# A planned attention and gMLP kernel: a second y3 buffer, transfers counted by the planner, chunk 0's load and scan, and the last outputs begun in part

## The chip, the cores and the metric

The kernel runs on one core of a Trainium2 chip. The metric is the device time of one execution in microseconds (us); a kernel's time is the median of its runs.

## The reference

For 4 batches and 8 heads of 48 dimensions over 768 positions the reference runs gated linear attention, and puts the result through a gated MLP with a spatial product:

```python
for t in range(S):
    state = alpha[:, :, t, :, None] * state + np.einsum('bhd,bhe->bhde', k[:, :, t], v[:, :, t])
    y[:, :, t] = np.einsum('bhd,bhde->bhe', q[:, :, t], state)
...
x = np.ascontiguousarray(attn_out.transpose(0, 2, 1, 3)).reshape(B, S, H * D)
h = x @ w_in
h = 0.5 * h * (1.0 + np.tanh(c * (h + 0.044715 * h ** 3)))
u, v = (h[..., :d_ff // 2], h[..., d_ff // 2:])
v_n = (v - mu) / np.sqrt(var + 1e-06) * g_ln
v_s = np.einsum('ts,bsd->btd', w_sg, v_n) + b_sg[None, :, None]
gated = u * v_s
return (x + gated @ w_out).astype(np.float32)
```

All is float32; d_model is 384 and d_ff is 1024. `mu` and `var` are the mean and variance of `v` over its 512 columns.

## The kernel before

**Attention.** The sequence of each batch is cut into 6 chunks of 128 positions; there are 24 chunks, 0 to 23, and a batch with its MLP is called a block. Chunk `i` loads `a` (decays, `load_a`) and `kqv` (768 KB, `load_kqv`). VectorE (DVE) scans the decays forward (`decay`, L333), scales the queries with the result `pf` (`scale_q`, L343), scans backward (`invert`, L351, into `pf` again) and scales the keys (`scale_k`, L361); `floor` is a small tile that L347 and L357 set between the scans. TensorE (PE) then works in groups G(o, i): the scores of chunk i (`sc`, L376), the outputs of chunk o (`y`, L389 and L399) and o's products of keys and values (`dl`, L410). VectorE masks the scores (`causal`, L475) and keeps the state: `state_half` (L495, or the copy L497 in the first chunk of a block), `state_add` (L500) and `state_decay` (L503). The second half of `y` reads `s_m`, which `state_half` writes.

**Between the two.** ScalarE (ACT) copies a chunk's `y` into the rows of `xf` and its last part into `y3` (`y_last`, L507). Six small DMAs, the packs (L520), put `y3` into the rest of `xf`. Then `xf` is split into a high part `xh` (L528) and a low part `xl` (L532).

**MLP.** A float32 product is made of three matmuls of high and low parts (`mm3`, L549 to L551). V(b, c) and U(b, hf, d) are the products with `w_in`; P(b, hf, d) is the spatial product (`mm_s`, 18 matmuls), whose result VectorE takes up (L630, then the gate L635, on GpSimd or VectorE) and splits into `gh` (L640) and `gl` (L645); R(b, hf, kk) is the output product (`mm_o`, 12 matmuls, the terms d = 0 to 3), followed by the add L663 into a tile `r` with two buffers, and its store L667. During block 0 the weights are split too: pieces of `w_in` and `w_out` pass ACT L247, DVE L250 to L269, ACT L263 and the lines L277 to L287, pieces of `w_sg` pass ACT L223 and DVE L226.

**Order.** Every engine works its queue off in order. The order is made when the program is built, by a list scheduler (`class Plan`): each step has an engine, a cost in ns, the steps that it follows, the tiles that it takes (with how many buffers, and who must be done before one comes free) and a due time. PE's steps have a fixed sequence, `units`, of which a step may be at most `ahead` places early; the other engines take of what is ready the step that is due first. A step marked `dve*` or `pool` may not run in the plan beside one on the other of these two engines, and some steps may go to either. All DMAs are issued by SyncE (SP), in its queue's order. In the program, each of SP's DMAs waits until the eighth one before it has landed; in the plan nothing stands for that.

## Time and profile before

| | us |
|---|---|
| median of 3 runs | 375.91 |
| lowest and highest | 375.25, 377.3 |
| the profiled execution, its own time | 374.54 |
| its span in the trace | 372.8 |
| TensorE busy in the span | 344.4 |
| VectorE busy | 265.1 |
| ScalarE busy | 152.8 |
| GpSimd busy | 60.6 |

The span leaves out 1.74 us of the execution's own time. Block 0 lasts to about 131 us: up to there the attention of two blocks, the first MLP and the weights' split share the engines. From there on TensorE waits little. To read the rows further below: a bracket such as [3.59 <-ACT y L507] says that the engine stood idle for 3.59 us before the instruction, and which instruction's end it waited for.

### The profile page before, as it was taken

Reading aid. Unit: us, or ns where it says so; the run is one execution under the profiler, and the core shown is the slowest. Engines: PE = TensorE matmul, PEld = TensorE weight load, DVE = VectorE, ACT = ScalarE, POOL = GpSimd, SP = SyncE. Lnnn points to the kernel's source line nnn. Section 1 sums busy time; section 2 is a strip of 40 time slices with the busy share of each in tenths; the row PEclk is TensorE's granted clock in tenths of the full one; section 3 lists DMA queues with packets and bytes.
Section 4 is the critical chain, followed back from the end, with each engine's and each line's share of the span. In section 5 each row is a group of like instructions: output and inputs, shape, how many; then the busy total and the mean of one; then the engine's idle time right before and its main releaser. Section 6 shows DMA issues by size and latency. Waiting matters only on the chain.

```text
span 372.8 us, 10703 instructions
## 1 busy us (share of the span) xinstructions
PE 344.4 (92%) x4480; PEld 314.3 (84%) x4480; DVE 265.1 (71%) x526; ACT 152.8 (41%) x367; POOL 60.6 (16%) x103
## 2 busy tenths in 40 slices
PE   2786989999998799999999999899999999999993
PEld 2554768799998798989999998699999989799983
DVE  4799997799996977888466887786577645443351
ACT  3285576755433344653312445543232335311010
POOL 1002133414201121320101301420111113300000
PEclk9999699999999999999999999999999999999998
DMA  8855675125356134531232344131221110000102
GB/s 304 281 195 139 218 250 181 42 73 163 98 170 205 31 111 122 162 114 37 66 117 93 119 138 136 52 101 28 92 83 73 30 50 8 1 2 0 63 3 70
DMA packets 18712, 39.38 MB, mean 106 GB/s; under 512 B 3936, under 2 KB 10848, under 8 KB 18656
## 3 DMA queue, kind: packets, MB, share of 16 engines
q1 hardware_dynamic: 18656, 38.61, 32.2%
q8 instruction: 37, 0.61, 0.7%
q14 instruction: 19, 0.16, 0.1%
HBM read 32.70 MB, written 4.72 MB: 100 GB/s over the span
## 4 chain that ended last, share of the span: by engine, by line
PE 68%; DVE 10%; DMA 8%; ACT 4%; SPq 4%; issue 3%; POOL 2%; DVEq 0%; ACTq 0%; POOLq 0%
PE mm_s L551 8%; PE mm_s L549 8%; PE mm_s L550 8%; DMA xf<-y 4%; PE mm_o L550 4%; PE mm_o L551 4%; PE mm_o L549 4%; PE mm_u L549 4%; SPq L520 4%; PE mm_u L551 4%; PE mm_u L550 4%; PE mm_v L549 3%; DMA kqv_t<-in_kqv 3%; PE mm_v L551 3%; PE mm_v L550 3%
## 5 line engine op out<-in xcount | busy, mean ns | idle before, releaser
L549 PE MATMUL mm_s<-ws_hi,vh 128*128 128x384 f32 x192 | 65.9, 343 | 1.3 <-ACT ws_hi L223 0.8
L550 PE MATMUL mm_s<-ws_lo,vh 128*128 128x384 f32 x192 | 65.1, 339 | 0.4 <-DVE ws_lo L226 0.4
L551 PE MATMUL mm_s<-ws_hi,vl 128*128 128x384 f32 x192 | 65.1, 339 | 0.1
L640 ACT CAST gh<-g 128x384 fp32r<-128x384 f32 x32 | 16.3, 512 | 57.9 <-DVE g L635 39.4
L630 DVE SCALAR_TENSOR_TENSOR g<-mm_s,g_col,b_bc 128x384 f32<-128x384 f32 x32 | 19.4, 608 | 26.1 <-PE mm_s L551 26.1
L549 PEld LDWEIGHTS mm_s<-ws_hi,vh 128*128 128x128 f32 x192 | 36.0, 188 | 2.1 <-ACT ws_hi L223 1.1
L550 PEld LDWEIGHTS mm_s<-ws_lo,vh 128*128 128x128 f32 x192 | 36.1, 188 | 0.8 <-DVE ws_lo L226 0.7
L551 PEld LDWEIGHTS mm_s<-ws_hi,vl 128*128 128x128 f32 x192 | 36.0, 188 | 0.4 <-DVE vl L596 0.4
L376 PE MATMUL sc<-kqv_t 64*64 64x64 f32 x768 | 27.8, 231 | 7.4 <-DVE kqv_t L361 4.7
L549 PE MATMUL mm_u<-xh,wi_hi 128*128 128x384 f32 x96 | 33.2, 346 | 0.1
L549 PE MATMUL mm_o<-gh,wo_hi 128*128 128x384 f32 x96 | 32.4, 338 | 0.3 <-ACT gh L640 0.3
L376 PEld LDWEIGHTS sc<-kqv_t 64*64 64x64 f32 x768 | 25.4, 146 | 8.5 <-DVE kqv_t L361 5.1
L550 PE MATMUL mm_o<-gl,wo_hi 128*128 128x384 f32 x96 | 32.4, 338 | 0.1
L550 PE MATMUL mm_u<-xl,wi_hi 128*128 128x384 f32 x96 | 32.5, 338 | 0.0
L551 PE MATMUL mm_u<-xh,wi_lo 128*128 128x384 f32 x96 | 32.4, 338 | 0.0
L551 PE MATMUL mm_o<-gh,wo_lo 128*128 128x384 f32 x96 | 32.3, 337 | 0.0
L549 PE MATMUL mm_v<-wi_hi,xh 128*128 128x512 f32 x72 | 30.3, 421 | 1.7 <-ACT u L615 1.4
L333 DVE TENSOR_TENSOR_SCAN pf<-a,floor 128x516 f32<-128x516 f32 x24 | 30.0, 1251 | 2.4 <-DMA a<-in_aT 2.2
L351 DVE TENSOR_TENSOR_SCAN pf<-a,floor 128x516 f32<-128x516 f32 x24 | 29.5, 1228 | 1.1 <-ACT pend L339 0.4
L551 PE MATMUL mm_v<-wi_hi,xl 128*128 128x512 f32 x72 | 28.5, 396 | 0.0
L550 PE MATMUL mm_v<-wi_lo,xh 128*128 128x512 f32 x72 | 28.4, 395 | 0.0
L389 PEld LDWEIGHTS y<-at,kqv_t 64*64 64x64 f32 x768 | 16.9, 141 | 13.2 <-issue 5.3
(109 smaller groups left out, 760.2 us busy)
## 6 DMA issues: line engine op xcount, KB each, us to landing
kqv_t<-in_kqv SPq DMA_DIRECT2D x24, 768.0 KB, 4.6
a<-in_aT SPq DMA_DIRECT2D x24, 258.5 KB, 2.7
out_x<-r SPq DMA_DIRECT2D x24, 192.0 KB, 2.5
raw<-in_w_in SPq DMA_DIRECT2D x8, 384.0 KB, 8.0
xf<-y SPq DMA_DIRECT2D x144, 8.0 KB, 2.7
raw<-in_w_out SPq DMA_DIRECT2D x4, 384.0 KB, 3.3
raw<-in_w_sgT SPq DMA_DIRECT2D x6, 192.0 KB, 2.4
raw_sg<-in_w_sgT SPq DMA_DIRECT2D x1, 768.0 KB
```

Of the source, the lines that this page charges most:

```text
L333: nc.vector.tensor_tensor_scan(pf.rearrange("p j t -> p (j t)"), s["a"][:, 0:NP * C1], floor.rearrange("p j t -> p (j t)"), initial=0.0, o ...
L351: nc.vector.tensor_tensor_scan(s["pf"].rearrange("p j t -> p (j t)")[:, ::-1], s["a"][:, NP * C1:0:-1], floor.rearrange("p j t -> p (j t)" ...
L376: lambda j=j, h=h: nc.tensor.matmul(sc[half(h), e, 64 * j:64 * j + 64], k[half(e), j, half(h)], q[half(e), j, half(h)], start=True, stop=True,
L389: lambda j=j: nc.tensor.matmul(y_of(y, j, e)[:, half(h)], v[half(h), j, half(e)], at[half(h), e, j], start=first and j < 2, stop=True, ski ...
L520: nc.sync.dma_start(xf[64 * e + D:64 * e + 64, kk, tsl], y3[64 * e + 16 * kk:64 * e + 16 * kk + 16, :])
L549: nc.tensor.matmul(o, lh, rh, start=(idx == 0), stop=False)
L550: nc.tensor.matmul(o, lh, rl, start=False, stop=False)
L551: nc.tensor.matmul(o, ll, rh, start=False, stop=(idx == n - 1))
L630: nc.vector.scalar_tensor_tensor(t["g"], t["o"], g_col[:, d:d + 1], b_bc[:, tsl], op0=ALU.mult, op1=ALU.add,)
L640: nc.scalar.copy(g["h"][:, d], t["g"])
```

## The change

The change has six parts.

1. The planner holds a DMA back until the eighth one before it has landed in its model (`SLOTS`). Only the order of the queues changes by it.
2. `y3` has two buffers: the copy of chunk i no longer has to follow the six packs of chunk i - 1.
3. Chunk 0's load of `kqv` is cut in two, keys and queries first (512 KB), then values (256 KB).
4. Chunk 0's backward scan writes into a tile `ip`, which is taken out of `xf`'s buffers, and no longer follows the scaling of the queries. In the plan, `pf` comes free when both q and k are scaled.
5. The copy of `state_half` in the first chunk of a block (four times) goes from VectorE to ScalarE.
6. Of the last three output products, the first two are begun with their first three terms d (9 matmuls each, `begin`), ahead of the last term (3 matmuls, `end`) of either; the third follows whole. In every output product the last term's three matmuls now stand in the order hi by `gh`, lo by `gh`, hi by `gl`.

```diff
     RATE = 280.0
+    SLOTS = 8
...
                     t1 = max(t, free[e])
+                    if s["nbytes"] and len(landed) >= self.SLOTS:
+                        t1 = max(t1, landed[-self.SLOTS])
...
                 done[n] = dma + 1900
+                landed.append(done[n])
...
-        nc.sync.dma_start(kqv_t, kqv[i])
+        if i == 0:
+            nc.sync.dma_start(kqv_t[:, 0:2], kqv[i, :, 0:2])
+            nc.sync.dma_start(kqv_t[:, 2], kqv[i, :, 2])
+        else:
+            nc.sync.dma_start(kqv_t, kqv[i])
...
     def invert(i):
         s = st[i]
+        if i == 0:
+
+            s["ip"] = mlp.tile([P, NK, TH], F32, tag="xf", name="ip", bufs=3).rearrange("p k t -> p (k t)")[
+                :, 0:NP * C1].rearrange("p (j t) -> p j t", t=C1)
+        else:
+            s["ip"] = s["pf"]
         nc.vector.tensor_tensor_scan(
-            s["pf"].rearrange("p j t -> p (j t)")[:, ::-1], s["a"][:, NP * C1:0:-1],
+            s["ip"].rearrange("p j t -> p (j t)")[:, ::-1], s["a"][:, NP * C1:0:-1],
...
-            nc.vector.tensor_copy(smd, d0)
+            nc.scalar.copy(smd, d0)
...
-        st[i]["y3"] = y3 = att1.tile([P, C], F32, tag="y3", name="y3")
+        st[i]["y3"] = y3 = att1.tile([P, C], F32, tag="y3", name="y3", bufs=2)
...
+        def begin():
+            t["o"] = psm.tile([P, TH], F32, tag="mm", name="mm_o")
+            terms = [(wo_hi[:, d, sl], wo_lo[:, d, sl], g["h"][:, d], g["l"][:, d]) for d in range(ND - 1)]
+            mm3(t["o"], terms, whole=False)
+
+        def end():
+            d = ND - 1
+            for lh, rh in ((wo_hi, "h"), (wo_lo, "h"), (wo_hi, "l")):
+                nc.tensor.matmul(t["o"], lh[:, d, sl], g[rh][:, d], start=False, stop=(rh == "l"))
...
         def product():
-            t["o"] = psm.tile([P, TH], F32, tag="mm", name="mm_o")
-            mm3(t["o"], [(wo_hi[:, d, sl], wo_lo[:, d, sl], g["h"][:, d], g["l"][:, d]) for d in range(ND)])
+            begin()
+            end()
...
-            units += p(b, 1, 0) + r(b, 0) + p(b, 1, 1) + p(b, 1, 2) + p(b, 1, 3) + r(b, 1)
+            units += p(b, 1, 0) + r(b, 0) + p(b, 1, 1) + p(b, 1, 2) + p(b, 1, 3)
+            units += [(("R", b, 1, kk, "begin"), 1560) for kk in range(2)] + r(b, 1)
...
-        plan.add(("recip", i), "dve*", 1225, lambda i=i: invert(i), [("q", i), ("pend", i), ("end", i)])
+        plan.add(("recip", i), "dve*", 1225, lambda i=i: invert(i), ([("q", i)] if i > 0 else []) + [("pend", i), ("end", i)])
...
-            ("half", i), "dve", 350, lambda i=i: state_half(i), [o_at[i]],
+            ("half", i), "dve" if c > 0 else "act", 350, lambda i=i: state_half(i), [o_at[i]],
```

Where the change moves instructions, three places of the queues are shown, before and after. Line numbers of the changed kernel lie 5 to 30 higher, since lines were added.

VectorE in the head, chunk 0, before (`pf` and `floor` as told above):

```order
L333 SCALAR_TENSOR_TENSOR pf<-a,floor 128x516
L347 RECIPROCAL floor<-pf 128x4
L343 TENSOR_TENSOR kqv_t<-kqv_t,pf 128x512
L351 SCALAR_TENSOR_TENSOR pf<-a,floor 128x516
L357 MEMSET floor 128x4
L361 TENSOR_TENSOR kqv_t<-kqv_t,pf 128x512
L475 TENSOR_TENSOR at<-sc,mask 128x512
```

and after:

```order
L342 SCALAR_TENSOR_TENSOR pf<-a,floor 128x516
L356 RECIPROCAL floor<-pf 128x4
L366 SCALAR_TENSOR_TENSOR ip<-a,floor 128x516
L372 MEMSET floor 128x4
L376 TENSOR_TENSOR kqv_t<-kqv_t,ip 128x512
L352 TENSOR_TENSOR kqv_t<-kqv_t,pf 128x512
L490 TENSOR_TENSOR at<-sc,mask 128x512
```

The scaling of the queries (L343, after L352) moved from ahead of the backward scan to behind the scaling of the keys (L361, after L376).

SyncE around the packs of chunk 5, before (`xf<-y_832` are the packs of chunk 4, `xf<-y_936` those of chunk 5; `raw` is a piece of a weight):

```order
L322 DMA a<-in_aT 128x517
L520 DMA xf<-y_832 16x128 x6
L243 DMA raw<-in_w_in 128x768
L327 DMA kqv_t<-in_kqv 128x1536
L243 DMA raw<-in_w_in 128x768
L520 DMA xf<-y_936 16x128 x6
L243 DMA raw<-in_w_out 128x768 x2
```

and after:

```order
L965 DMA g_col<-in_g_ln 128x4
L336 DMA kqv_t<-in_kqv 128x1536
L327 DMA a<-in_aT 128x517
L535 DMA xf<-y_832 16x128 x6
L535 DMA xf<-y_915 16x128 x6
L248 DMA raw<-in_w_in 128x768 x2
L336 DMA kqv_t<-in_kqv 128x1536
L327 DMA a<-in_aT 128x517
L248 DMA raw<-in_w_out 128x768 x2
```

The packs of chunk 5 (after: `xf<-y_915`) moved ahead of the load of chunk 8's `kqv` and of both pieces of `w_in`, right behind those of chunk 4.

VectorE ahead of the first half of the state of chunk 7, which is the row `s_m<-s_c,dl_1451`, before:

```order
L347 RECIPROCAL floor<-pf 128x4
L635 TENSOR_TENSOR g<-g,u 128x384
L284 TENSOR_TENSOR top<-top,wo_hi 128x384
L266 TENSOR_SCALAR mag<-top 128x384
L269 SCALAR_TENSOR_TENSOR mag<-raw,mag 128x384 x2
L287 TENSOR_TENSOR wo_lo<-top,mag 128x384
L495 TENSOR_TENSOR s_m<-s_c,dl_1451 128x4x48
L475 TENSOR_TENSOR at<-sc,mask 128x512
L645 TENSOR_TENSOR gl<-g,gh 128x384 x2
L343 TENSOR_TENSOR kqv_t<-kqv_t,pf 128x512
```

and after, where it is the row `s_m<-s_c,dl_1466` (L645 is before's L630, L650 is L635, L660 is L645, L352 is L343, L366 is L351, L231 is L226, L292 is L287):

```order
L289 TENSOR_TENSOR top<-top,wo_hi 128x384
L645 SCALAR_TENSOR_TENSOR g<-mm_s,g_col,b_bc 128x384
L292 TENSOR_TENSOR wo_lo<-top,mag 128x384
L650 TENSOR_TENSOR g<-g,u 128x384
L352 TENSOR_TENSOR kqv_t<-kqv_t,pf 128x512
L231 TENSOR_TENSOR ws_lo<-raw,ws_hi 128x384
L660 TENSOR_TENSOR gl<-g,gh 128x384
L366 SCALAR_TENSOR_TENSOR pf<-a,floor 128x516
L510 TENSOR_TENSOR s_m<-s_c,dl_1466 128x4x48
L231 TENSOR_TENSOR ws_lo<-raw,ws_hi 128x384
L376 TENSOR_TENSOR kqv_t<-kqv_t,pf 128x512
L515 TENSOR_TENSOR s_m<-s_m,sc 128x4x48
```

The scaling of chunk 8's queries, its backward scan and a piece of `w_sg` moved from behind this row to ahead of it, two more low halves `gl` are done ahead of it, and a gate (L635) and three of the low parts of `w_out` (L287), which GpSimd made before, are VectorE's now.

## Rows read from the trace of the kernel before

**Rows 1.** The page, its row of busy times: busy us, share of the span and number of instructions of each engine.

```profile
PE 344.4 (92%) x4480; PEld 314.3 (84%) x4480; DVE 265.1 (71%) x526; ACT 152.8 (41%) x367; POOL 60.6 (16%) x103
```

**Rows 2.** The view by windows over the whole span, cut at the stages of block 0 and the rest: window, its length, then busy us (and instructions) of PE, PEld, DVE, ACT and POOL, the granted TensorE clock as a share of full speed, the busy share of the DMA engines, GB/s.

```profile
20.00:36.00 16.00, 13.24 (x290) 9.70 (x290) 15.29 (x30) 11.71 (x33) 1.88 (x1) 1.00 0.53 166
36.00:50.00 14.00, 11.86 (x263) 9.60 (x263) 13.83 (x27) 7.40 (x19) 1.72 (x1) 0.76 0.60 197
50.00:72.00 22.00, 20.41 (x176) 15.99 (x176) 17.65 (x43) 15.53 (x35) 9.16 (x16) 1.00 0.55 174
72.00:88.00 16.00, 16.00 (x116) 14.82 (x115) 15.67 (x34) 10.20 (x24) 3.52 (x4) 1.00 0.21 59
88.00:102.00 14.00, 14.00 (x301) 13.37 (x300) 13.32 (x31) 6.72 (x18) 4.95 (x4) 1.00 0.49 151
```

**Rows 3.** The same view in finer windows around TensorE's longest wait.

```profile
36.00:38.00 2.00, 0.00 (x0) 0.00 (x0) 2.00 (x6) 1.40 (x4) 0.12 (x1) 0.56 0.80 203
...
42.00:43.00 1.00, 1.00 (x5) 0.89 (x4) 1.00 (x1) 0.15 (x1) 0.00 (x0) 0.50 0.09 17
```

**Rows 4.** The timeline of VectorE in the head, chunk 0: start, duration, engine, line, operation, out<-in, shapes, count, and in brackets the idle time before it with what ended it.

```profile
5.09 0.18 DVE L347 RECIPROCAL floor<-pf 128x4 f32<-128x4 f32 x1
5.71 0.69 DVE L343 TENSOR_TENSOR kqv_t<-kqv_t,pf 128x512 f32<-128x512 f32 x1 [0.44 <-DMA kqv_t<-in_kqv]
6.51 1.23 DVE L351 TENSOR_TENSOR_SCAN pf<-a,floor 128x516 f32<-128x516 f32 x1
7.79 0.68 DVE L361 TENSOR_TENSOR kqv_t<-kqv_t,pf 128x512 f32<-128x512 f32 x1
```

**Rows 5.** The timeline of TensorE, the rows before which it waits and that the prediction speaks of (at 100.31 it doesn't wait).

```profile
8.53 0.70 PE L376 MATMUL sc<-kqv_t 64*64 64x64 f32 x16 [4.35 <-DVE kqv_t L361]
...
38.02 0.39 PE L389 MATMUL y<-at,kqv_t 64*64 64x64 f32 x4 [3.59 <-ACT y L507]
...
67.50 0.50 PE L549 MATMUL mm_v<-wi_hi,xh 128*128 128x512 f32 x1 [0.30 <-ACT xh L528]
...
100.31 0.41 PE L399 MATMUL y<-kqv_t,s_m 64*64 64x64 f32 x16
...
114.61 0.45 PE L549 MATMUL mm_s<-ws_hi,vh 128*128 128x384 f32 x1 [0.76 <-ACT ws_hi L223]
...
115.49 0.44 PE L550 MATMUL mm_s<-ws_lo,vh 128*128 128x384 f32 x1 [0.43 <-DVE ws_lo L226]
...
128.93 0.46 PE L389 MATMUL y<-at,kqv_t 64*64 64x64 f32 x16 [1.44 <-ACT alo L454]
...
130.22 0.46 PE L399 MATMUL y<-kqv_t,s_m 64*64 64x64 f32 x16 [0.59 <-DVE s_m L495]
```

**Rows 6.** The timeline of SyncE's queue of DMA issues, at the loads ahead of chunk 5's packs, and at the load of chunk 11.

```profile
57.73 0.52 SPq L243 DMA_DIRECT2D raw<-in_w_in  x1
...
110.62 1.84 SPq L220 DMA_DIRECT2D raw<-in_w_sgT  x2
...
113.02 0.38 SPq L327 DMA_DIRECT2D kqv_t<-in_kqv  x1
```

**Rows 7.** The timeline of ScalarE at chunk 5's y3 and xh.

```profile
59.15 0.27 ACT L507 COPY y<-y 128x128 f32<-128x128 f32 x1 [1.30 <-DMA xf<-y]
...
66.94 0.51 ACT L528 CAST xh<-xf 128x384 fp32r<-128x384 f32 x1 [1.37 <-DMA xf<-y]
```

**Rows 8.** The timeline of VectorE, at the first half of the state of chunk 7 and at the queries of chunk 11.

```profile
99.61 0.35 DVE L495 TENSOR_TENSOR s_m<-s_c,dl 128x192 f32<-128x192 f32 x1
...
119.31 0.70 DVE L343 TENSOR_TENSOR kqv_t<-kqv_t,pf 128x512 f32<-128x512 f32 x1 [1.77 <-DMA kqv_t<-in_kqv]
```

**Rows 9.** VectorE by line: line, engine, operation, out<-in, shapes, count | busy us, mean ns of one | idle before, and releasers.

```profile
L645 DVE TENSOR_TENSOR gl<-g,gh 128x384 fp32r<-128x384 f32 x32 | 17.6, 555 | 9.1 <-ACT gh L640 8.8
...
L343 DVE TENSOR_TENSOR kqv_t<-kqv_t,pf 128x512 f32<-128x512 f32 x24 | 16.5, 686 | 5.1 <-DMA kqv_t<-in_kqv 4.9
...
L635 DVE TENSOR_TENSOR g<-g,u 128x384 f32<-128x384 f32 x25 | 14.7, 587 | 0.5
...
L226 DVE TENSOR_TENSOR ws_lo<-raw,ws_hi 128x384 fp32r<-128x384 f32 x6 | 3.4, 598 | 0.5 <-ACT ws_hi L223 0.4
...
L497 DVE COPY s_m<-dl 128x192 f32<-128x192 f32 x4 | 1.4, 358 | 1.9 <-PE dl L410 1.9
L287 DVE TENSOR_TENSOR wo_lo<-top,mag 128x384 fp32r<-128x384 f32 x1 | 0.6, 550 | 0.0
```

**Rows 10.** The timeline of TensorE at the last three output products: the first and the last of the first nine matmuls, the tenth, and the last of all.

```profile
359.58 0.34 PE L549 MATMUL mm_o<-gh,wo_hi 128*128 128x384 f32 x1
...
360.99 0.34 PE L551 MATMUL mm_o<-gh,wo_lo 128*128 128x384 f32 x1
361.58 0.45 PE L549 MATMUL mm_o<-gh,wo_hi 128*128 128x384 f32 x1 [0.26 <-ACT gh L640]
...
366.62 0.34 PE L551 MATMUL mm_o<-gh,wo_lo 128*128 128x384 f32 x1
```

**Rows 11.** The timeline of VectorE there, the first and the last of the three adds.

```profile
362.83 0.56 DVE L663 TENSOR_TENSOR r<-mm_o,xf 128x384 f32<-128x384 f32 x1 [0.71 <-PE mm_o L551]
...
366.99 0.56 DVE L663 TENSOR_TENSOR r<-mm_o,xf 128x384 f32<-128x384 f32 x1 [1.53 <-PE mm_o L551]
```

**Rows 12.** The view of DMA from 360 us on, its last row: the stores of these three, KB each, median us from issue to landing.

```profile
out_x<-r SPq DMA_DIRECT2D x3, 192.0 KB, 3.0
```

More of the change, by code (lines that the diff above doesn't have):

```diff
@@ L97, in issue @@
         dma = 0.0
+        landed = []
         while left:
@@ L360, in scale_k @@
         s = st[i]
-        eng.tensor_tensor(s["k"], s["k"], s["pf"][:, :, 1:], op=ALU.mult)
+        eng.tensor_tensor(s["k"], s["k"], s["ip"][:, :, 1:], op=ALU.mult)
     def range_low(i):
@@ L544, in x_second, with mm3 @@
         x_low(x["xf"], x["xh"], x["xl"], i % NCH, eng)
-    def mm3(o, terms):
-        n = len(terms)
+    def mm3(o, terms, whole=True):
+        n = len(terms) + (not whole)
         for idx, (lh, ll, rh, rl) in enumerate(terms):
@@ L655, in mlp_out @@
         t = {}
+        def begin():
[6 more added lines that the diff above has]
+                nc.tensor.matmul(t["o"], lh[:, d, sl], g[rh][:, d], start=False, stop=(rh == "l"))
+        t["parts"] = begin, end
         def product():
-            t["o"] = psm.tile([P, TH], F32, tag="mm", name="mm_o")
-            mm3(t["o"], [(wo_hi[:, d, sl], wo_lo[:, d, sl], g["h"][:, d], g["l"][:, d]) for d in range(ND)])
+            begin()
+            end()
         def add():
@@ L667, in store @@
             nc.sync.dma_start(dst, t["r"])
-        return [("pe", 2080, product), ("dve", 525, add), ("sp", 370, store)]
+        return [("pe", 2080, product), ("dve", 525, add), ("sp", 370, store), t["parts"]]
     def general_chunk(state, i, x_all):
@@ L693, in general_chunk @@
         x = att1.tile([P, NK, C], F32, tag="kn", name="gx")
-        y3 = att1.tile([P, C], F32, tag="y3", name="gy3")
+        y3 = att1.tile([P, C], F32, tag="y3", name="gy3", bufs=2)
         nc.scalar.copy(y3, y[:, NP - 1, 0:C])
@@ L723, in general_mlp @@
             for kk in range(NK):
-                run(mlp_out(g, x[hf], b, hf, kk))
+                run(mlp_out(g, x[hf], b, hf, kk)[:3])
     plan = Plan()
@@ L855, in tile_gla_gmlp @@
         plan.add(("kqv", i), "sp", 330, lambda i=i: load_kqv(i), takes=[("kqv", 3, [("H",) + o_at[i][1:]])], nbytes=786432)
-        plan.add(("scan", i), "dve*", 1225, lambda i=i: decay(i), [("a", i)] + ([("floor", i - 1)] if i > 0 else []), takes=[("pf", 1, [("k", i)])])
+        plan.add(("scan", i), "dve*", 1225, lambda i=i: decay(i), [("a", i)] + ([("floor", i - 1)] if i > 0 else []), takes=[("pf", 1, [("q", i), ("k", i)])])
         plan.add(("pend", i), "act", 200, lambda i=i: decay_end(i), [("scan", i)])
@@ L885, in tile_gla_gmlp @@
         head = i % CPH == 0
-        plan.add(("y3", i), "act", 275, lambda i=i: y_last(i), [ended], takes=[("y3", 1, [("pack", i, kk, e) for kk in range(NK) for e in range(2)])])
+        plan.add(("y3", i), "act", 275, lambda i=i: y_last(i), [ended], takes=[("y3", 2, [("pack", i, kk, e) for kk in range(NK) for e in range(2)])])
         plan.add(
@@ L991, in tile_gla_gmlp @@
                 deps = [("P", b, hf, d, 4) for d in range(ND)] + (pieces_of("wo") if b == 0 else [])
-                plan.add(r, *st_[0], deps, [("mm", 3, [r + ("add",)])], due=due[r])
+                if (b, hf) == (B - 1, 1) and kk < 2:
+                    begin, end = st_[3]
+                    first = r + ("begin",)
+                    plan.add(first, "pe", 1560, begin, deps[:ND - 1], [("mm", 3, [r + ("add",)])], due=due[first])
+                    plan.add(r, "pe", 520, end, deps + [first], due=due[r])
+                else:
+                    plan.add(r, *st_[0], deps, [("mm", 3, [r + ("add",)])], due=due[r])
                 plan.add(r + ("add",), *st_[1], [r], [("r", 2, [r + ("store",)])], soon=(r, 4000))
```

## The prediction

> **What bounds the kernel now.** I read the row of busy times first: TensorE works 344.4 of 372.8 us [rows 1], so 28.4 us of idle time is all that can be won without less work for it. Next come the windows [rows 2]: from 72 to 102 us TensorE never waits, while between 36 and 50 us VectorE is busy 13.83 of 14 us and TensorE is the one that waits. VectorE is the second bound, and in block 0 the two change places. Then the timeline of TensorE names the single waits [rows 5]: 3.59 us at 38.02, 0.30 at 67.50, 0.76 and 0.43 at 114.61 and 115.49, 1.44 and 0.59 at 128.93 and 130.22. The change speaks to these, to the wait of 4.35 us for the first scores, and to the last outputs. After 131 us the order of the queues is almost the same in both kernels.
>
> The sum is made against the profiled execution, 374.54 us (372.8 of span and 1.74 around it). The median of the runs, 375.91, lies 1.37 above it; I take the sum as a difference and add it to the median. About 0.5% (1.88 us) is what a measurement of this kernel tells from no change, so "same" is 374.03 to 377.79.
>
> **Part by part: the head and the wait at 38.02.** In the new order VectorE's backward scan of chunk 0 follows the small reciprocal of 5.09, which ends at 5.27, and no longer waits 0.44 us for the load and 0.69 for the queries [rows 4]. The scan then runs from about 5.33 instead of 6.51, and keys follow it. Keys arrive in the same load as queries, at 5.71, before the scan ends at 6.56; so cutting the load in two is hidden, and one more issue on SyncE costs the next load some 0.4 us, which nothing waits for. The queries are now scaled behind the keys: the gain for the first scores is not 1.18 but 1.18 less 0.69, which is 0.49 us.
>
> The copy of the state (0.358 us [rows 9]) leaves VectorE as well, at chunk 0. Together VectorE is 0.80 us earlier. The wait of 3.59 us ends with ScalarE's copy of y3, which the second buffer frees. But in the rows of that wait VectorE is busy 2.00 of 2 us [rows 3], and from 36 to 50 us it has 0.17 us of idle time [rows 2]; the group of products behind the wait also needs chunk 4's keys, which that same VectorE makes, and the weights' pieces after them. So the wait gets shorter, and TensorE waits later for VectorE instead. What arrives at 48 us is VectorE's own lead. I take -0.6 us of its 0.80. Bounds: 0, if the lead is lost to the weights' order, and -1.7, if VectorE also loses the 0.71 and 0.17 us that it idles between 20 and 50 us [rows 2]. TensorE's granted clock is 0.50 until 43 us after this wait (1.2 of 2.4 GHz) [rows 3]; a shorter wait may keep it up, but with VectorE full in the same rows that is not added.
>
> **The packs of chunk 5.** Before, y3 of chunk 5 waits 1.30 us, and the packs stand behind two weight loads and a load of kqv; xh starts at 66.94 [rows 7], the first of those loads at 57.73 [rows 6], and TensorE waits 0.30 us at 67.50. In the new order the packs come ahead of all three. This takes away the 0.30, and no more, since TensorE is busy up to there: -0.3 (bounds 0 and -0.3). What waits instead are the two weight pieces, which the new order of TensorE wants later too.
>
> **72 to 102 us: VectorE has more ahead.** Counted from the order, ahead of the first half of chunk 7's state there now stand one scaling of queries (0.69), one backward scan (1.23, as at 6.51 [rows 4]), one piece of w_sg (0.60), one gate (0.59), two low halves (1.11) and three low parts of w_out (1.65), less two copies (0.72): 5.15 us by their durations [rows 4, 9]. Before, this instruction runs at 99.61 and ends at 99.96 [rows 8], and the matmuls that read it start at 100.31 [rows 5]: 0.35 us of slack. Up to 4.8 us could become a wait of TensorE. Against it stands idle time which the work can fill: VectorE idles 4.35 us between 50 and 72 us and 0.33 between 72 and 88 [rows 2], and the new order puts chunk 7's scans and scalings between the norms of V, where this idle time is. I take 3.0 of the 4.7 as filled: 4.8 less 3.0 is +1.8 us. Bounds: 0 (all filled) and +4.8.
>
> **102 to 131 us: waits that should go.** Pieces of w_sg are loaded from 110.62 on [rows 6], and TensorE waits for them 0.76 and 0.43 us. In the new order their loads and splits start ahead of the output stores: -1.2. Chunk 11's kqv is issued at 113.02, behind two such loads of 1.84 us, and VectorE waits 1.77 us for it at 119.31 [rows 6, 8]; TensorE's 1.44 and 0.59 us follow from that chain. Without the two loads ahead, 1.84 of these 2.03 can go. Together -3.0. Bounds: -3.2 (all four) and -1.2 (the load of kqv still late, since its buffer comes free only with the products of chunk 8).
>
> **131 us to the end.** The state's copy on ScalarE, which is busy 152.8 of 372.8 us [rows 1], costs 0 to 0.2 us four times; I take 0. The last outputs: nine matmuls from 359.58 to 360.99 have a pitch of 0.176 us [rows 10]; begun for two products, 18 of them cover the wait for the last gate, and all 36 would be issued by 359.58 + 35 x 0.176 = 365.74 instead of 366.62, 0.88 us earlier. The first product, though, now ends with the 21st matmul, which starts at 363.10, and an add starts 0.37 us after its last matmul (366.62 to 366.99), so the first add starts at 363.47 instead of 362.83 [rows 11]. Its store follows 0.56 us later at 364.03 and lands in 3.0 us [rows 12], at 367.03. The tile r has two buffers: the third add writes into the first one's and starts at 367.0, as before at 366.99. So I take 0 for this part. Bounds: -0.9 (the store lands early enough, and TensorE's end decides) and +0.1.
>
> A page of the Trainium skill would have it otherwise: "DMA: Bandwidth & Descriptors", in its anatomy of one DMA, gives a fixed cost of about 2.0 us and a rate of 436 GB/s, from which 196,608 bytes take an estimated 2.45 us. By it the third add starts at about 366.5 and the sum is 0.5 lower; the last stores of this trace, with 3.0, don't agree, and I go by them.
>
> **The sum.** -0.6 - 0.3 + 1.8 - 3.0 + 0 = -2.1 us: 372.4 for the profiled execution's own time, 373.8 for the median.
>
> **Rivals.** First, slower: VectorE is late at chunk 7. The price is the whole +4.8, and the load of chunk 11 stays late (-1.2 in place of -3.0): -0.6 - 0.3 + 4.8 - 1.2 = +2.7, 378.6. It decides when TensorE's new waits from 68 to 102 us pass 1.88 + 0.6 + 0.3 + 1.2, about 4.0 us. For it: VectorE's 15.67 of 16 us from 72 to 88, and that a GpSimd step has become its own. Against it: 4.7 us of idle time ahead. Chance 0.17.
>
> Second, nothing that can be measured: the waits change their names. VectorE's extra work returns what the earlier loads give, the y3 wait is hidden behind VectorE, the tail behind the store: -0.6 - 0.3 + 3.2 - 3.0 = -0.7, 375.2. For it: VectorE is full on both sides of each wait that goes. Chance 0.33.
>
> Third, a large gain: VectorE's idle time takes all the added work, the clock stays up and all four later waits go: -1.7 - 0.3 + 0 - 3.2 - 0.9 = -6.1, 369.8. It needs VectorE to have less than 1 us of idle time from 50 to 88. Chance 0.13.
>
> **How the numbers follow.** My forecast, 373.8, has a chance of 0.37; its own spread reaches across 374.03, so I give 0.33 of it to faster and 0.04 to same. Faster: 0.33 + 0.13 and 0.02 of the second rival's lower edge, 0.48; same: 0.04 + 0.31 = 0.35; slower 0.17. The range goes from 370.0 to 378.4: the prices of the third rival below and of the first above lie at its ends, and less than 2 in 10 is left out.
>
> **What would show it.** Right: the first scores start near 8.05; the wait at 38 is shorter, but V of block 0 starts only some 0.6 us earlier; no wait for w_sg near 114; xh of chunk 5 starts about 3 us earlier; the third add starts at 367 in the old time, released by a DMA. Wrong: TensorE waits for s_m or a VectorE row between 68 and 102 us by more than 4 us in all (first rival), or by nothing (third); or VectorE isn't full from 26 to 48 us, so that the whole 3.59 us is won.

## The result, and the profile after

The changed kernel takes 376.64 us (median of 20 runs, 375.01 to 379.46), the kernel before 375.17 on the same chip (20 runs, 371.3 to 378.73): 1.0065 times as long, 95% interval 1.0038 to 1.0092. I had predicted 373.8 and faster; it is 0.65% slower, and the time lies inside the range of 370.0 to 378.4. The ratio, here and below, takes of each kernel only the runs within 1.5% of its fastest one, which leaves out two runs of the kernel before and none of the change; over all 20 runs each the medians differ by 1.47 us, 0.39%. Single runs scatter over 4 to 8 us, so the smaller differences below are read from traces and not from times.

The profiled execution of the change took 376.72 us, with a span of 375.0: 2.2 us more than before. Its row of busy times, which answers to [rows 1]:

```profile
PE 347.7 (93%) x4480; PEld 316.6 (84%) x4480; DVE 264.0 (70%) x522; ACT 156.7 (42%) x374; POOL 54.8 (15%) x100
```

TensorE idles 27.3 us instead of 28.4 and is still slower, since it is busy 3.3 us longer with the same 4480 matmuls. Where this happens is seen when both spans are cut at the same three points of the program: the end of block 0's first V product (V starts at 45.52 before and at 44.83 after), the end of G(7,8) (the attention's products of chunk 7 with the scores of chunk 8 among them), and the end of G(9,10). Between the cuts both kernels run 611, 697, 382 and 2796 matmuls (one that lies across a cut counts on both sides). The view by windows, before and then after, columns as in [rows 2]:

```profile
0.00:48.10 48.10, 32.99 (x611) 25.20 (x615) 40.07 (x79) 24.63 (x66) 5.30 (x15) 0.93 0.68 232
48.10:101.32 53.22, 51.52 (x697) 45.14 (x698) 47.72 (x106) 33.18 (x74) 17.62 (x24) 1.00 0.41 128
101.32:131.28 29.96, 26.74 (x382) 25.26 (x382) 25.67 (x48) 11.13 (x30) 3.63 (x3) 1.00 0.43 131
131.28:372.80 241.52, 233.16 (x2796) 218.66 (x2795) 151.63 (x295) 83.81 (x198) 34.02 (x61) 1.00 0.23 72
```

```profile
0.00:47.40 47.40, 33.92 (x611) 25.21 (x614) 40.02 (x78) 25.01 (x67) 4.51 (x15) 0.93 0.69 235
47.40:107.99 60.59, 55.73 (x697) 47.48 (x698) 52.02 (x116) 35.92 (x80) 13.23 (x21) 0.94 0.37 116
107.99:133.73 25.74, 25.74 (x382) 25.11 (x382) 21.84 (x42) 9.59 (x25) 3.87 (x4) 1.00 0.46 144
133.73:375.00 241.27, 232.35 (x2796) 218.79 (x2795) 150.10 (x290) 86.16 (x202) 33.22 (x61) 0.99 0.23 72
```

The four stretches change by -0.70, +7.37, -4.22 and -0.25 us, together +2.20. The loss is all in the second. There TensorE idles 4.86 us instead of 1.70 (+3.16) and is busy 4.21 longer, and the granted clock is 0.94 instead of 1.00. VectorE is busy 4.30 longer and idles 8.57 us instead of 5.50. The third stretch gains more than predicted: TensorE doesn't wait in it at all. In the second and third together VectorE is busy 73.86 us instead of 73.39 and idles 12.47 instead of 9.79: the new order moved its work ahead, and what was added is mostly idle time. These are one trace of each kernel; how far another trace of either would differ is told with e1 below.

The timeline of TensorE after, at the rows that answer to [rows 5] and at the new waits:

```profile
7.80 1.13 PE L391 MATMUL sc<-kqv_t 64*64 64x64 f32 x32 [3.62 <-DVE kqv_t L352]
...
34.87 0.46 PE L404 MATMUL y<-at,kqv_t 64*64 64x64 f32 x16 [1.28 <-ACT y L522]
37.34 0.37 PE L391 MATMUL sc<-kqv_t 64*64 64x64 f32 x1 [1.91 <-DVE floor L372]
...
54.01 0.46 PE L404 MATMUL y<-at,kqv_t 64*64 64x64 f32 x16 [0.98 <-ACT y L522]
...
57.39 0.63 PE L566 MATMUL mm_v<-wi_hi,xl 128*128 128x512 f32 x1
...
78.61 0.44 PE L564 MATMUL mm_s<-ws_hi,vh 128*128 128x384 f32 x1 [2.13 <-ACT vh L607]
...
79.42 0.44 PE L566 MATMUL mm_s<-ws_hi,vl 128*128 128x384 f32 x1 [0.19 <-DVE vl L611]
...
80.31 1.48 PE L280 MATMUL mm_w<-top,ident 128*128 128x384 f32 x2
...
106.94 0.46 PE L414 MATMUL y<-kqv_t,s_m 64*64 64x64 f32 x16 [0.31 <-DVE s_m L510]
```

First scores start at 7.80 instead of 8.53. The wait of 3.59 us has become one of 1.28 for ScalarE's y3 and one of 1.91 for VectorE. At 78.61 the first spatial product of block 0 (P0 below) waits 2.13 us for `vh`, the high part of the last two normed V. Behind it, and behind the wait at 54.01, matmuls take longer: 0.63 us for a row of mm_v that takes 0.40 at 46.06, and 1.48 for the pair at 80.31 that takes 0.81 at 20.81. The windows there have a granted clock of 0.58 and 0.55, mostly 1.2 of 2.4 GHz:

```profile
56.30:60.30 4.00, 4.00 (x18) 3.10 (x11) 3.33 (x8) 2.95 (x6) 2.40 (x3) 0.58 0.08 16
79.90:83.70 3.80, 3.80 (x10) 2.59 (x9) 3.80 (x8) 0.99 (x3) 0.00 (x0) 0.55 0.31 103
```

At full clock those 7.8 us would be 4.0 x 0.58 + 3.8 x 0.55 = 4.4, so by this estimate 3.4 of the 4.21 us are clock.

The rows of VectorE and then ScalarE that stand behind P0's wait and behind 106.94:

```profile
70.28 1.29 DVE L611 TENSOR_TENSOR vl<-vg,vh 128x512 fp32r<-128x512 f32 x2 [1.70 <-ACT vh L607]
...
78.07 1.29 DVE L611 TENSOR_TENSOR vl<-vg,vh 128x512 fp32r<-128x512 f32 x2 [1.79 <-ACT vh L607]
...
106.55 0.33 DVE L510 TENSOR_TENSOR s_m<-s_c,dl 128x192 f32<-128x192 f32 x1
```

```profile
69.65 1.12 ACT L607 CAST vh<-vg 128x512 fp32r<-128x512 f32 x2
...
71.39 1.06 ACT L579 ACTIVATE vg<-mm_v 128x512 f32<-128x512 f32 x2
...
76.72 0.81 ACT L599 ACTIVATE vg<-vg,off,rstd 128x512 f32<-128x512 f32 x1 [1.82 <-POOL off L596]
77.44 1.12 ACT L607 CAST vh<-vg 128x512 fp32r<-128x512 f32 x2
```

Each row "x2" is a pair: the planner now norms V of chunks 2 and 3 together, and those of 4 and 5. Before, the casts to `vh` stand singly, between the gelus of the chunks that follow. `vg` has two buffers, so the gelus of 4 and 5 (71.39) can't start before the pair 2, 3 is split; then everything of 4 and 5 is late. VectorE idles 1.70 us for the casts of 2 and 3, and 1.79 us for those of 4 and 5. From 78.07 on its rows show no gap up to 106.55, the first half of chunk 7's state, for which TensorE waits.

The last outputs, VectorE's adds, which answer to [rows 11]:

```profile
365.47 1.09 DVE L690 TENSOR_TENSOR r<-mm_o,xf 128x384 f32<-128x384 f32 x2 [1.36 <-PE mm_o L680]
369.07 0.56 DVE L690 TENSOR_TENSOR r<-mm_o,xf 128x384 f32<-128x384 f32 x1 [2.51 <-DMA out_x<-r]
```

The third add is released by the DMA of the first one's store and not by TensorE, as predicted: 365.47 + 0.56 + 3.0 [rows 12] is 369.03, and the row has 369.07.

### The profile page after: what moved, and what is told of

It reads as the page before. It is cut to its first block, busy times and chain, and to the rows that moved or that the text cites. A ratio compares the mean times of both kernels' runs of the same rounds, so it can differ in the third digit from the quotient of the medians.

```text
span 375.0 us, 10715 instructions
## 1 busy us (share of the span) xinstructions
PE 347.7 (93%) x4480; PEld 316.6 (84%) x4480; DVE 264.0 (70%) x522; ACT 156.7 (42%) x374; POOL 54.8 (15%) x100
## 4 chain that ended last, share of the span: by engine, by line
PE 68%; DVE 15%; issue 4%; POOL 3%; ACT 3%; DMA 3%; SPq 2%; DVEq 0%; ACTq 0%; POOLq 0%
PE mm_s L566 8%; PE mm_s L564 8%; PE mm_s L565 8%; PE mm_o L566 3%; PE mm_o L565 3%; PE mm_o L564 3%; PE mm_v L564 3%; PE mm_o L680 3%; PE y L404 3%; PE mm_v L565 3%; PE mm_v L566 3%; PE mm_u L564 3%; PE mm_u L565 3%; PE mm_u L566 3%; PE tp L485 2%
## 5 line engine op out<-in xcount | busy, mean ns | idle before, releaser
L645 DVE SCALAR_TENSOR_TENSOR g<-mm_s,g_col,b_bc 128x384 f32<-128x384 f32 x32 | 19.5, 611 | 27.5 <-PE mm_s L566 27.5
L342 DVE TENSOR_TENSOR_SCAN pf<-a,floor 128x516 f32<-128x516 f32 x24 | 29.4, 1224 | 2.3 <-DMA a<-in_aT 2.1
L366 DVE TENSOR_TENSOR_SCAN pf<-a,floor 128x516 f32<-128x516 f32 x23 | 28.3, 1228 | 0.8 <-ACT pend L348 0.3
L583 DVE BATCH_NORM_STATS2 stats<-vg 128x6 f32<-128x512 f32 x24 | 16.4, 688 | 14.4 <-ACT vg L579 14.4
L404 PE MATMUL y<-at,kqv_t 64*64 64x64 f32 x768 | 22.6, 231 | 2.6 <-ACT y L522 2.5
L690 DVE TENSOR_TENSOR r<-mm_o,xf 128x384 f32<-128x384 f32 x24 | 13.0, 551 | 16.1 <-PE mm_o L680 13.6
```

Source lines behind the costliest of these rows:

```text
L342: nc.vector.tensor_tensor_scan(pf.rearrange("p j t -> p (j t)"), s["a"][:, 0:NP * C1], floor.rearrange("p j t -> p (j t)"), initial=0.0, o ...
L366: nc.vector.tensor_tensor_scan(s["ip"].rearrange("p j t -> p (j t)")[:, ::-1], s["a"][:, NP * C1:0:-1], floor.rearrange("p j t -> p (j t)" ...
L404: lambda j=j: nc.tensor.matmul(y_of(y, j, e)[:, half(h)], v[half(h), j, half(e)], at[half(h), e, j], start=first and j < 2, stop=True, ski ...
L583: nc.vector.bn_stats(t["stats"], t["vg"])
L645: nc.vector.scalar_tensor_tensor(t["g"], t["o"], g_col[:, d:d + 1], b_bc[:, tsl], op0=ALU.mult, op1=ALU.add,)
L690: nc.vector.tensor_tensor(t["r"], t["o"], x["xf"][:, kk], op=ALU.add)
```

## The experiments

Two questions: are the changed instructions slow, or the order that the planner makes with them; and in that order, does VectorE or TensorE's clock set the end of G(7,8). "Before" always means runs on the same chip.

**The change's instructions in the order of before** (e1), and the same with a third buffer for the last add (e2). The planner is told of none of parts 1 to 5, and chunk 0's scaling of the queries is put behind that of its keys by hand. The lines of parts 3 and 4 are those of the change and aren't shown again.

```diff
-        st[i]["y3"] = y3 = att1.tile([P, C], F32, tag="y3", name="y3")
+        st[i]["y3"] = y3 = att1.tile([P, C], F32, tag="y3", name="y3", bufs=2)
...
-            nc.vector.tensor_copy(smd, d0)
+            nc.scalar.copy(smd, d0)
...
+            t["o"] = psm.tile([P, TH], F32, tag="mm", name="mm_o")
+            terms = [(wo_hi[:, d, sl], wo_lo[:, d, sl], g["h"][:, d], g["l"][:, d]) for d in range(ND - 1)]
+            mm3(t["o"], terms, whole=False)
```

and e2 besides:

```diff
-            t["r"] = mlp.tile([P, TH], F32, tag="r", name="r", bufs=2)
+            third = isinstance(b, int) and (b, hf, kk) == (B - 1, 1, 2)
+            t["r"] = mlp.tile([P, TH], F32, tag="g" if third else "r", name="r", bufs=2)
```

> All six parts' instructions, issued in the order that the kernel before has (the planner sees the old rules; only chunk 0's scaled queries follow the keys, the state's copies run on ScalarE, y3 has its second buffer, and the last outputs are begun in part). Theory A, the loss is the new order of block 0: this is 0.3 to 1.2 us faster than before (ratio 0.997 to 0.999), with no wait of TensorE for vh and no new fall of its clock between 50 and 90 us. Rival B, the new instructions themselves cost (the second buffer, ScalarE's copies, the cut load): as slow as the change, ratio 1.004 to 1.008.

> As the kernel in the old order, and the last add writes into a tile of another tag instead of the two r buffers. If the store of the first output holds the third add, the third add starts about 0.9 us earlier against the end of TensorE's work than with two buffers, and the time is 0.6 to 1.0 us below that of the old order with two buffers. If TensorE's end or the first add decides, both are equal within 0.2 us.

e1: 375.47 us (before 374.55), 1.0024 (0.9977 to 1.0071); e2: 375.81, 0.9971 (0.9911 to 1.0031). Neither can be told from before, but the interval of e1 holds the change's 1.0065 too, so these times alone don't settle the question. The traces do better. e1 has no wait for `vh`, and from 48 to 102 us its clock is 1.00. The trace to set beside it is that of e16 (below): it has the order of before and, up to 104 us, the instructions of before. The second stretch, of e16 and then of e1:

```profile
49.47:104.47 55.00, 52.12 (x698) 45.46 (x698) 48.77 (x107) 33.39 (x74) 17.48 (x24) 1.00 0.41 125
```

```profile
48.97:103.55 54.58, 51.85 (x697) 45.09 (x698) 47.66 (x106) 33.61 (x75) 17.62 (x24) 1.00 0.41 125
```

The first three stretches take 49.47, 55.00 and 30.31 us in e16, and 48.97, 54.58 and 30.72 in e1. So in block 0 the instructions cost nothing that shows; the new order does. The same traces show how far one trace can be trusted: with the instructions of before, e16 is 1.78 us longer than the trace of before in the second stretch (53.22). In the old order that stretch takes 53.22 to 55.00 us (before, e1, e2, e16), with VectorE idle for 5.50 to 6.92; in the change's order (after, e12, e15) it takes 60.47 to 60.59, with VectorE idle for 8.46 to 8.57. The third takes 29.96 to 30.72 and 25.74 to 26.36. The loss in the second is therefore 5.5 to 7.4 us, the gain in the third 3.6 to 5.0.

But TensorE's long wait at 38 us stays in e1, with two buffers of y3. Rows of ScalarE and TensorE of e1:

```profile
37.45 0.72 ACT L378 ACTIVATE a<-a,alo 128x512 f32<-128x512 f32 x1 [1.08 <-DVE pf L362]
...
38.60 0.26 ACT L520 COPY y<-y 128x128 f32<-128x128 f32 x1
```

```profile
38.91 0.70 PE L402 MATMUL y<-at,kqv_t 64*64 64x64 f32 x16 [3.61 <-ACT y L520]
```

The copy stands in ScalarE's queue behind a step that waits 1.08 us for VectorE's scan. It was this place in the queue that made it late, and not the packs of the chunk before. Where the planner knows of the second buffer, it puts the copy earlier, and the wait is 1.28 us, in the change (34.87) as in e5 below.

**One part at a time, each with the order that the planner makes of it**: y3 alone (e5), the count of transfers alone (e6), and parts 3 to 5 (e7: head and state copy).

```diff
-        plan.add(("y3", i), "act", 275, lambda i=i: y_last(i), [ended], takes=[("y3", 1, [
+        plan.add(("y3", i), "act", 275, lambda i=i: y_last(i), [ended], takes=[("y3", 2, [
```

```diff
+    SLOTS = 8
...
+                    if s["nbytes"] and len(landed) >= self.SLOTS:
+                        t1 = max(t1, landed[-self.SLOTS])
```

```diff
-        plan.add(("recip", i), "dve*", 1225, lambda i=i: invert(i), [("q", i), ("pend", i), ("end", i)])
+        plan.add(("recip", i), "dve*", 1225, lambda i=i: invert(i), ([("q", i)] if i > 0 else []) + [("pend", i), ("end", i)])
...
-            ("half", i), "dve", 350, lambda i=i: state_half(i), [o_at[i]],
+            ("half", i), "dve" if c > 0 else "act", 350, lambda i=i: state_half(i), [o_at[i]],
```

> The kernel before with y3's second buffer alone, known to the plan, which makes its own order: the fifth V product stands right behind the fourth as in the change, but a piece of w_in and a U product come ahead of the first spatial product, and ScalarE's steps of the norms of V are not in pairs from the third V on. Theory A', the change loses by the paired norms (both norms of a pair on ScalarE, then both high parts) together with the spatial product that is put ahead of the last of them: no wait over 1 us for vh here, ratio to before 0.996 to 1.003. Rival B, the second buffer and what it lets in costs by itself: 1.004 to 1.008.

> The kernel before with the transfers counted in the plan alone. Its own order: the fifth V product behind a piece and the scores, norms of V one after the other. Theory A': no wait over 1 us for vh, ratio 0.995 to 1.003. Rival: the count of transfers spoils the order, a wait of over 1 us for vh or for a piece, ratio over 1.004.

> The kernel before with chunk 0's cut load and moved scan and with ScalarE's copies, in the plan's own order; the norms of the third and fourth V are in a pair, those of the last two are not. Theory A' and the head's price (first scores 0.5 to 0.75 us earlier, of which VectorE keeps the most): ratio 0.996 to 1.001, first scores near 7.8 to 8.1. Rival: the lead is lost by 30 us, and the pair costs over 1 us at the first spatial product: 1.002 to 1.006.

e5: 387.56 us (before 375.66), 1.0386 (1.0334 to 1.0439). e6: 374.77, 1.0047 (1.0004 to 1.0091). e7: 381.76, 1.0225 (1.0162 to 1.0288). e5 and e7 are slower than all six parts together. Of e6 the times leave it open: by its median it is 0.89 us below before, by the ratio above it. The largest waits of TensorE in e5, e6 (from 110 us on) and e7:

```profile
76.43 0.44 PE L276 MATMUL mm_w<-wi_hi,nident 128*128 128x384 f32 x1 [1.92 <-ACT wi_hi L263]
...
127.39 0.44 PE L549 MATMUL mm_s<-ws_hi,vh 128*128 128x384 f32 x1 [3.57 <-ACT ws_hi L223]
```

```profile
129.40 0.46 PE L394 MATMUL y<-at,kqv_t 64*64 64x64 f32 x16 [0.49 <-ACT alo L459]
```

```profile
39.84 0.70 PE L399 MATMUL y<-at,kqv_t 64*64 64x64 f32 x16 [6.32 <-ACT y L517]
```

In e5 no wait is for `vh`; the weights' pieces come late instead, and the clock is 0.57 from 77 to 85 us. My theory and its rival both missed the times of e5 and e7. e6 shows what the count of transfers does by itself: the waits of 0.76 and 0.43 us for w_sg [rows 5] shrink to 0.15, and 1.44 to 0.49.

**P0 later** (e3) and **V of chunk 5 later** (e8), in the change: if P0 merely stands too early in TensorE's queue, other work ahead of it should cover the wait.

```diff
+                    deps += [("low_pe", "wu", 2)] if (hf, d) == (0, 0) else []
```

and in e8 V of chunk 5 follows `("low_pe", "wu", 1)`, the second such piece.

> The change, with one dependency more in the plan: the first spatial product of block 0 follows the third U piece of w_in on TensorE. Theory A in its narrow form (the loss is the place of this product: a wait of 2.1 us for vh, and the fall of the clock behind it): the wait goes, no fall of the clock at 80 us, 2.5 to 4 us faster than the change, ratio to before 0.994 to 0.999. Rival C (the norms of V are paired, so vh comes late whatever stands there): the wait moves to the next product that needs vh, and the time stays within 1 us of the change.

> The change, with one dependency more in the plan: the sixth V product of block 0 follows the second U piece of w_in, which makes ScalarE take the norms of the last V products one after the other, and puts a U product ahead of the first spatial product. Theory A': the wait of 2 us for vh goes, 1.5 to 3 us faster than the change, ratio to before 0.998 to 1.002. Rival C (any order of the change's plan meets late norms or pieces): a wait of 2 us or more for vh, a U piece or w_sg between 60 and 115 us, ratio 1.005 or more.

e3: 385.82 us (before 374.55), 1.0309 (1.0255 to 1.0364); e8: 380.55 (before 375.66), 1.0204 (1.0145 to 1.0263). P0's wait for `vh` is gone in both, but others have come, here of e3 and of e8:

```profile
79.65 0.44 PE L566 MATMUL mm_u<-xh,wi_lo 128*128 128x384 f32 x1 [3.83 <-ACT wi_lo L285]
...
126.42 0.69 PE L564 MATMUL mm_s<-ws_hi,vh 128*128 128x384 f32 x1 [3.84 <-ACT ws_hi L228]
```

```profile
121.26 0.45 PE L564 MATMUL mm_s<-ws_hi,vh 128*128 128x384 f32 x1 [2.93 <-ACT ws_hi L228]
```

One more dependency reorders all of block 0, so these two runs say nothing of what P0's wait is worth. In e9, e10, e14, e17 and e18 the order is therefore edited step by step, with all else left in its place.

**The tail of the change with a third buffer** (e4; the edit of e2), and all six parts, with that buffer, in the order that the count of transfers alone gives (e11).

> The change, with the last add in a tile of another tag instead of the two r buffers. Same order of all queues. If the store holds the third add, it is 0.8 to 1.0 us faster than the change (ratio to before about 1.004 where the change has 1.0065). If not, the same.

> The order that the plan makes when it counts transfers and knows nothing else of the change (the run with the count of transfers alone), with the instructions of all other parts placed in that order, and the last add in a third tile. The order theory: 0.5 us (head) and 0.9 us (third tile) below the run with the count alone, ratio to before 0.993 to 1.001. If the instructions cost by themselves: 1.003 or more.

e4: 376.08 us (before 374.55), 1.0069 (1.0029 to 1.0109); e11: 376.04 (before 375.74), 1.0009 (0.9965 to 1.0053). VectorE's last adds in e4:

```profile
364.77 1.09 DVE L691 TENSOR_TENSOR r<-mm_o,xf 128x384 f32<-128x384 f32 x2 [1.36 <-PE mm_o L680]
367.42 0.56 DVE L691 TENSOR_TENSOR r<-mm_o,xf 128x384 f32<-128x384 f32 x1 [1.56 <-PE mm_o L680]
```

The third add follows the first by 2.65 us instead of 3.60, and TensorE releases it: the 0.9 us that I had as the bound of this term are there, once the tile r isn't short. The median doesn't show them. In **the tail on the kernel before** (e16: part 6 and the third buffer alone) the third add starts 0.37 us after the last matmul, as expected, and the time can't be told from no change either: 374.47 (before 374.61), 0.9976 (0.9923 to 1.0030).

> The kernel before in its own order, with the last outputs begun in part and the last add in a third tile: in its trace the third add starts 0.35 to 0.4 us after the last matmul and is not released by a DMA; 0.6 to 1.0 us below before, ratio 0.997 to 0.9985, which the scatter of single runs may hide.

**Norms one after another** (e9): the change's emitted order with ten steps of the norms of chunks 2 and 5 moved, so that the pairs fall apart; e10 adds the third buffer, and e12 is the change again on their chip.

```diff
+MOVES = [(('V', 0, 2, 7), ('V', 0, 3, 6)), (('V', 0, 2, 8), ('recip', 7)), (('V', 0, 5, 1), ('V', 0, 3, 7)),
...
+        for n, place in MOVES:
+            k = [j for j, m in enumerate(made) if m[0] == n][0]
+            step = made.pop(k)
+            made.insert([j for j, m in enumerate(made) if m[0] == place][0], step)
```

> The change, every queue in its own order but for ten steps of the norms of V in block 0: high and low part of the third V ahead of the norm of the fourth, and gelu, statistics, norm, high and low part of the sixth V (in this plan it goes ahead of the fifth) ahead of those of the fifth. TensorE's and SyncE's queues are the change's, row by row. Theory A' (the paired norms and the spatial product in front of them cost the 2.1 us of waiting for vh, and the clock's fall behind it): vh of the last V comes 1.5 to 3 us earlier, the wait at the first spatial product falls below 0.6 us, and the time is 1.5 to 4 us below the change. Rival C (the wait moves on to the next piece): the product starts without a wait but TensorE waits for a U piece or a gate before 95 us instead, within 1 us of the change.

> The kernel with the norms in turn, and the last add in a tile of another tag than the two r buffers. If both work as the traces have it: 0.9 us below the one with the norms in turn, 2.4 to 5 us below the change, ratio to before 0.990 to 1.000. If theory A' falls: about 0.9 us below the change.

> The change itself, on the same chip as the three others, to compare with them directly. Ratio to before 1.002 to 1.009; the same two places of the trace: TensorE waits about 2 us for vh near 78 us, and its clock falls behind that; a fall near 56 us in some executions only.

e9: 374.78 us (before 375.74), 1.0048 (1.0016 to 1.0080); e10: 375.09, 1.0041 (1.0007 to 1.0074); e12: 376.51, 1.0089 (1.0055 to 1.0122). Against the change beside them, e9 is 1.7 us shorter and e10 1.4, less than the 2.4 to 5 expected of e10. But P0's wait is still 1.45 us where I expected less than 0.6:

```profile
74.57 0.44 PE L576 MATMUL mm_u<-xh,wi_lo 128*128 128x384 f32 x1 [1.61 <-ACT wi_lo L295]
79.63 0.45 PE L574 MATMUL mm_s<-ws_hi,vh 128*128 128x384 f32 x1 [1.45 <-ACT vh L617]
```

The second stretch takes 60.12 us in e9 and 59.15 in e10, against 60.47 in e12. So the pairs are a part of the loss, 0.4 to 1.3 us of it by these traces, and not all of it.

**The wait filled** (e13): 34 small products of a constant, which nothing reads, stand in P0 ahead of the part that waits, so that TensorE isn't idle there. e15 is the change on that chip, e14 is e10 with 24 such products.

```diff
+                if s == NS - 2:
+                    for _ in range(fill):
+                        nc.tensor.matmul(spare[:, 0:P], warm, warm, start=True, stop=True)
```

> The change in its own order on every engine, with 34 matmuls of 128 columns on a constant (into a PSUM tile that nobody reads) put into the first spatial product of block 0, where TensorE waits some 2 us for vh. They change no output and cost TensorE about 2 us of time in which it waits anyway. Theory D, the fall of the clock behind that wait is caused by the idle time in it and costs about 2 us: no fall between 79 and 84 us, TensorE's next products at full speed, 1.5 to 2.5 us below the change. Rival E, the clock falls there whatever TensorE does in the wait, or the fall is made up for later: a fall between 78 and 85 us, within 0.7 us of the change.

> The kernel with the norms in turn and a third tile for the last add, with 24 of the same matmuls in the same place. If theories A' and D hold and add up: no fall of the clock near 80 us, 3.5 to 5.5 us below the change, ratio to before 0.988 to 0.998. If the clock's fall stays: as the kernel without the filling, 1.4 to 2 us below the change.

> The change once more, beside the two kernels with the wait filled, on the same chip: ratio to before 1.003 to 1.010, a fall of the clock behind the wait near 78 us in the profiled execution.

e13: 376.49 us (before 374.61), 1.0097 (1.0067 to 1.0128); e14: 375.29, 1.0045 (1.0001 to 1.0088), which is less of a gain than expected; e15: 378.12, 1.0145 (1.0078 to 1.0212). The window from 80 to 82 us in e13 and in e15:

```profile
80.00:82.00 2.00, 2.00 (x10) 1.60 (x10) 2.00 (x4) 0.20 (x1) 0.00 (x0) 1.00 0.34 94
```

```profile
80.00:82.00 2.00, 2.00 (x8) 1.39 (x7) 2.00 (x4) 0.32 (x2) 0.00 (x0) 0.59 0.49 127
```

The filled wait leaves the clock at 1.00. But TensorE then waits for VectorE at 107.40:

```profile
107.40 0.46 PE L414 MATMUL y<-kqv_t,s_m 64*64 64x64 f32 x16 [1.29 <-DVE s_m L510]
```

From the restart of P0 to the end of G(7,8) both take 29.36 us (79.09 to 108.45, and 78.77 to 108.13). So the slow clock at 80 us costs nothing net: VectorE sets this end. The 1.6 us between the medians of e13 and e15 (12 and 6 runs) aren't in this stretch, and I can't place them: the two profiled executions took 376.86 and 377.08.

**The state's first half earlier** (e17): e13 with chunk 9's scaling of queries and backward scan moved right behind that instruction; e18 has all of it (norms in turn, filled wait, state first, third buffer).

```diff
+MOVES = [(('q', 9), ('low', 'ws', 1, 1)), (('recip', 9), ('low', 'ws', 1, 1))]
```

> The change with the wait filled by 34 matmuls, and two steps of VectorE moved from ahead of the first half of chunk 7's state to right behind it: the scaling of chunk 9's queries and its backward scan (0.69 and 1.23 us). Nothing else moves. Theory F, VectorE is busy without a gap from the late vh near 78 us to this step, so that it, not TensorE's clock, sets the group G(7, 8): TensorE's wait for s_m (1.29 us with the wait filled) falls below 0.3 us, G(7, 8) ends about 1 us earlier against the first spatial product than with the filling alone, and no wait for chunk 9's keys comes in its place. Time 2 to 3 us below the change (ratio to before 1.000 to 1.005). Rival G: what is moved is needed soon after, the scores of chunk 9 or the masks wait for it by 1 us or more, and the time is that of the filling alone (1.006 to 1.010).

> All that the runs point to in one kernel on the change's order: norms in turn, the wait filled (24 matmuls), chunk 9's queries and backward scan behind the first half of chunk 7's state, and the last add in a third tile. If the terms add up: 4 to 5.5 us below the change, ratio to before 0.990 to 1.000. If VectorE still sets G(7, 8) or the scatter covers it: 1.000 to 1.005.

e17: 376.92 us (before 372.36), 1.0112 (1.0056 to 1.0169); e18: 373.64, 1.0028 (0.9997 to 1.0059). In e17 the wait for s_m is gone and the stretch takes 27.85 us instead of 29.36: it shows that VectorE's two added steps set it. The work moved is then late for chunk 9:

```profile
115.90 0.46 PE L414 MATMUL y<-at,kqv_t 64*64 64x64 f32 x16 [0.90 <-ACT alo L479]
```

and the third stretch takes 26.87 us instead of the 25.76 of e13: 1.1 of the 1.5 us are given back. The time is no lower. e18, with every repair, has the lowest ratio among the versions in the change's order, and no version is measurably faster than the kernel before.

## Why the prediction was wrong

A correction first: in the rows ahead of chunk 7's first half, the added scaling of queries and backward scan are those of chunk 9; the text ahead of the prediction ascribes them to chunk 8. Their cost is the same.

- **Head and the wait at 38 (-0.6).** Right in size: -0.70. The first scores gained 0.73 us, a little more than the 0.49 predicted, and VectorE's lead is what arrived at V. The reason I gave for the old wait was wrong: e1 shows that a second buffer alone doesn't shorten it, and e5 that the copy's earlier place in ScalarE's queue does.
- **Packs of chunk 5 (-0.3).** Right: xh starts 2.6 us earlier, at 64.31, and TensorE no longer waits for it there. Not predicted: behind a wait of 0.98 us at 54.01, V of chunk 2 runs at half clock in the profiles of after, e12 and e15, and not in e4, e10 or e13.
- **72 to 102 us (+1.8): the step that failed.** The work was sized about right, 5.15 us predicted and 4.30 measured up to the end of G(7,8). What failed is "I take 3.0 of the 4.7 as filled". VectorE's idle time there didn't shrink, it grew by 3.07 us (by 1.5 at least between any two traces of the old and the new order), in part since the same new order pairs the norms, and with them VectorE waits for ScalarE at 70.28 and 78.07; with the pairs undone it idles 7.94 us there in e9 and 6.94 in e10, against 8.57. The stretch from the first V product to the end of G(7,8) is 7.37 us longer (5.5 at least), beyond my bound of +4.8, which assumed that idle time could only be filled. e9 and e10 show that part of it is the pairing, e13 that the slow clock at 80 us is no cost of its own, e17 that VectorE sets its end. Which steps of the new order make up the rest of the 7.37 is not shown.
- **102 to 131 us (-3.0).** Right: the four waits, 3.22 us in all, are gone, and e6 shows three of them shorter with the count of transfers alone. The stretch is 4.22 us shorter. The other 1.0 is TensorE's busy time, 25.74 us instead of 26.74 for the same 382 matmuls. VectorE has 3.83 us less to do here, and that is the work which the new order put into the stretch before.
- **The tail (0).** Right, and for the reason given. By the fixed cost and rate in the Trainium skill, "DMA: Bandwidth & Descriptors", anatomy of one DMA, the store would take an estimated 2.45 us and the third add start near 368.5; the trace has 369.07, in line with the 3.0 us of [rows 12]. This isn't evidence against the page: that section gives its figures for transfers that GpSimd issues, and these stores are SyncE's, so they should not have been used here.
- **The rivals.** The first was the mechanism: VectorE late at chunk 7. It had its place right but not how it came about, and its other half, a late load of chunk 11, didn't happen: +7.37 and -4.22 stand where it had +4.8 and -1.2. Its sign, more than 4 us of new waits of TensorE, did not show either: from 68 us to the end of G(7,8) they come to 2.9, and much of the delay stands in the trace as busy time at half clock (the 3.4 us above, over the whole stretch). At 378.6 it was 2.0 above the median, nearer than my 373.8, and 0.17 was too small a chance for it. In its favour I had listed VectorE's 15.67 of 16 us; against it idle time that a list of added rows can't show to be free. The second rival's 375.2 lay nearest, 1.4 below, but by luck: it has +3.2 and -3.0 where +7.37 and -4.22 stand.

Open: how much of the 0.65% is the half clock of V of chunk 2 (from V's start to P0's restart it takes 33.7 to 33.8 us in after, e12 and e15, which have it, and 33.0 to 34.3 in e4, e13 and e17, which don't); why the median of e17 isn't 0.4 us lower, which is what the trace leaves of its gain; and what most of the scatter of single runs is. Of 147 runs of the kernel before, 69 are under 375.0 us; of 38 of the change, none.

## What to carry to other kernels

With a planner, an edit is its instructions plus a new order of everything. Replay the old order with the new instructions, and the new order with a few steps moved, before you cost the parts: here the instructions were worth nothing that could be measured and single parts in an order of their own cost up to 3.9%. And take more than one trace of the kernel before: two executions of the same order differed by 1.8 us in the stretch in question.

When the next engine in line is near full, count its idle time in the new order and ask whom each gap waits for; idle time is free for added work only if the steps that end the gap come no later than before. Before a tile gets a second buffer, look at what stands ahead of its writer in the writer's own queue.
